# Storing the first chunk's scores by rows in an attention and expert kernel, and letting the first loads wait for their own rows

## The chip, the cores and the metric

The kernel runs on one core of one Trainium2 chip. The metric is the device time of one execution in microseconds (us). Times of the kernel before are the median of three runs.

## What is computed

Attention whose heads are mixed before and after the softmax, for 4 batches, 12 heads, 448 positions and 64 elements a head, and then a feed-forward product of two weight matrices with a gate between them:

```python
scores = scale * np.matmul(q, k.transpose(0, 1, 3, 2))
scores = np.einsum('bhij,hg->bgij', scores, w_pre)
scores = scores - np.max(scores, axis=-1, keepdims=True)
attn = np.exp(scores)
attn = attn / (np.sum(attn, axis=-1, keepdims=True) + 1e-09)
attn = np.einsum('bhij,hg->bgij', attn, w_post)
x = np.matmul(attn, v)              # then (b, i, h*d): 1792 x 768
h = x @ w_in                        # 768 x 2048
out = (h * np.clip(h + 3.0, 0.0, 6.0) / 6.0) @ w_out
```

## The kernel before

**Tiling.** Each batch's 448 rows of scores are cut into four chunks (120, 120, 120 and 90 rows, the last with two rows of padding). A chunk's scores are computed head pair by head pair with all rows on the partitions, but the mix of the heads wants the twelve heads of a few rows on the partitions. So the scores go through DRAM: a chunk is written there as `sd` (row, head, column), and read back as `T_all`, ten rows times twelve heads on the partitions. One load (line 491) brings twenty rows, two "steps" of ten; six loads make a chunk of 120 rows. A step is: first mix (PE, line 499), negated maximum (DVE, 506), exponent and sum (ACT, 507), scaling of the sum and of the exponents (POOL and DVE, 509 to 515), second mix (PE, 534), copy into the chunk's `A` (ACT and DVE, 543 and 545). When a chunk's `A` is full, it is multiplied with `v` (line 571), and two chunks together are the tokens of one pass of the experts' first product (line 769), which ends the start of the program.

**The first chunk.** `first_scores` (line 412) treats chunk 0 of batch 0 apart: each pair's two heads are copied out of PSUM by ACT (line 423) and DVE (line 424) into one buffer `S0` of all twelve heads, and each pair is stored by a transfer of its own, 120 rows of two heads (line 425). The load of step `s` lists the whole `sd` among what it reads, so every load of chunk 0 waits for all six stores.

**What runs beside it.** `w_in` comes in sixteen items of 768 KB (line 662), each decoded from 64-bit numbers by one pass on ACT (617) and DVE passes (620 to 632) before it is split into two halves of 16 bits. `v` comes in four loads. PE, when the planner sees it idle between 9 and 150 us of its own reckoning, is given filler matmuls on the identity (line 808).

**What sets the order.** All instructions are written down first as operations with an engine, a duration, what they read and write, and a priority; `Plan.schedule` (line 171) then places them one by one, each engine taking the operation of lowest priority value among those that are ready by its reckoning, and `Plan.run` (line 268) keeps the best of 128 such orders. An engine executes its list in order; so does SP, which issues every transfer here. An operation in another's `order` list may not start before that other one has started; one in its `succ` list, not before it has ended. Because the order is planned anew, a changed operation at the start can move rows anywhere in the program.

The store of a pair, and what a load of step `s` waits for:

```python
dma(CI * 3584, lambda: SP.dma_start(sd()[:, h:h + 2], S0()[:, h:h + 2]),
    [(S0, h), (S0, h + 1)], [(sd, pr)], at + 0.7)            # line 425
t_load[s] = dma(215040 * R, lambda: SP.dma_start(
    T_all()[4:4 + HR * R, slot], sd()[i0:i0 + 10 * R].rearrange("(u r) h j -> (r h) u j", u=2)),
    [sd, T_all], [T], s - 2.5)                               # line 491
```

Of the kernel before, what the change touches and what calls it, by code (L numbers as in the profile page):

```python
# [28 lines left out]
CI = 120  # L29
# [7 lines left out]
HR = G5 * H  # L37
# [10 lines left out]
LATE_W = 'P4', 'P5', 'P3'  # L48
HALF, W_AT, W_BY, EARLY, V_AT = 8, 20, 6, 1, 2
POST16 = 24  # L50
FILL_FROM, FILL_TO = 9, 150
WO_EARLY, WO_AT, WO_BY = 24, 72, 4
NH = S // 2
# [230 lines left out]
def body(ctx: ExitStack, tc: tile.TileContext, q4, kT, vj, wpre0, wpost0, ident0, w_in, w_out, outT):  # L284
    nc = tc.nc
    PE, ACT, DVE, POOL, SP = nc.tensor, nc.scalar, nc.vector, nc.gpsimd, nc.sync
# [19 lines left out]
    def buf(pool, shape, dt, tag, name, bufs=1, ring=True):  # L306

        g = rings.setdefault((id(pool), tag), Ring(bufs)) if ring else None
        return Buf(lambda: pool.tile(shape, dt, tag=tag, name=name, bufs=bufs), g)

    def const(shape, dt, name, pool=keep):
        return Buf(lambda: pool.tile(shape, dt, name=name))

    def act(dur, fn, r, w, prio):
        return plan.op("ACT", dur, fn, r, w, prio)

    def dve(dur, fn, r, w, prio, share=False):
        return plan.op("DVE", dur, fn, r, w, prio, share=share)

    def pool(dur, fn, r, w, prio):  # L320
        return plan.op("POOL", dur, fn, r, w, prio)

    def pe(dur, fn, r, w, prio, after=(), mode=0):
        return plan.op("PE", dur, fn, r, w, prio, after, 0, mode)

    def dma(nbytes, fn, r, w, prio, after=()):
        return plan.op("SP", 0.5, fn, r, w, prio, after, nbytes)
# [15 lines left out]
    def place(places):  # L343
        z = Buf(None)
        z.pool = places
        return z
# [53 lines left out]
    S0 = buf(apool, [CI, H, S], F32, "A", "s0", 2)  # L400

    def products(q, k, pr, at):

        def mm():
            for c, m in ((0, D), (D, CI - D)):
                for u in range(2):
                    r = slice(u * D, u * D + D)
                    PE.matmul(at[u]()[c:c + m], q()[r, pr, c:c + m], k()[r, pr % 3, :], start=True, stop=True)  # L408

        return mm  # L410

    def first_scores(pr, at):
        sd, q, k = s_dram[0, 0], qs[0, 0], ks[0, pr // 3]
        if pr % 3:
            ps = [place(singles) for u in range(2)]
            at2 = [lambda u=u: ps[u]()[:, :S] for u in range(2)]
        else:
            two = place(pairs)
            ps = [(two, 0), (two, 1)]
            at2 = [lambda u=u: two()[:, u, :S] for u in range(2)]  # L420
        pe(0.77, products(q, k, pr, at2), [(k, pr % 3), q], ps, at, mode=1)
        h = 2 * pr
        act(0.45, lambda: ACT.activation(S0()[:, h], at2[0]()[:CI], AF.Copy), [ps[0]], [(S0, h)], at + 0.5)
        dve(0.55, lambda: DVE.tensor_copy(S0()[:, h + 1], at2[1]()[:CI]), [ps[1]], [(S0, h + 1)], at + 0.5)
        dma(CI * 3584, lambda: SP.dma_start(sd()[:, h:h + 2], S0()[:, h:h + 2]), [(S0, h), (S0, h + 1)], [(sd, pr)], at + 0.7)


    s_dram, last_qk = {}, []
# [1 line left out]
    def scores(b, c, pr, at):  # L430
        n = CH[c]
        if pr == 0:
            s_dram[b, c] = Buf(lambda: dsc.tile([CI, H, S], F32, name=f"sd_{b}_{c}"))
        if (b, c) == (0, 0):
            return first_scores(pr, at)
        sd, q, k = s_dram[b, c], qs[b, c], ks[b, pr // 3]
        ps = place(pairs)
        last_qk[:] = [pe(0.77, products(q, k, pr, [lambda u=u: ps()[:, u, :S] for u in range(2)]), [(k, pr % 3), q], [ps], at, last_qk, mode=1)]
        st = buf(rot, [CI, 2, S], F32, "s", f"s_{b}_{c}_{pr}", 2)
        act(0.82, lambda: ACT.activation(st()[:n], ps()[:n, :, :S], AF.Copy), [ps], [st], at + 0.5)  # L440
        dma(n * 3584, lambda: SP.dma_start(sd()[:n, 2 * pr:2 * pr + 2], st()[:n]), [st], [(sd, pr)], at + 0.7)
# [33 lines left out]
    A, t_load = {}, {}  # L475

    def step(s):


        b, t = divmod(s, STEPS)  # L480
        c = min(t // 12, 3)
        t -= 12 * c
        if t % 2:
            t_load[s] = t_load[s - 1]
            return
        i0 = t * SI
        R = 2 if t < NST[c] - 1 else 1
        slot = s // 2 % NT_BUFS
        T = Buf(None, rings.setdefault(("T", slot), Ring(1)))
        sd = s_dram[b, c]  # L490
        t_load[s] = dma(215040 * R, lambda: SP.dma_start(
            T_all()[4:4 + HR * R, slot], sd()[i0:i0 + 10 * R].rearrange("(u r) h j -> (r h) u j", u=2)), [sd, T_all], [T], s - 2.5)
        ps = [place(mixed) for r in range(R)]

        def pre():
# [7 lines left out]
        pe(0.39 * R, pre, [T, wpre8], [*ps, (e, "pe")], s - 0.7, mode=1)  # L503
        eh, el = (buf(rot, [P, 2, S], F16, x, f"{x}_{s}", 2) if s >= POST16 else None for x in ("eh", "el"))
        for r in range(R):
# [8 lines left out]
        for r in range(R):  # L514
            pool(0.63, lambda r=r: POOL.tensor_scalar(e()[:, r], e()[:, r], rr()[:, r:r + 1], 1.0, op0=ALU.mult, op1=ALU.mult), [rr], [(e, r)], s + 0.6 + 0.3 * r)  # L515
            if s >= POST16:
                act(0.47, lambda r=r: ACT.activation(eh()[:, r], e()[:, r], AF.Copy), [(e, r)], [(eh, r)], s + 0.65 + 0.3 * r)  # L517
                pool(1.02, lambda r=r: POOL.tensor_tensor(el()[:, r], e()[:, r], eh()[:, r], op=ALU.subtract), [(e, r), (eh, r)], [(el, r)], s + 0.7 + 0.3 * r)  # L518
        if s < POST16:
            mix, dur = [(e, wpost_n)], 1.05  # L520
# [272 lines left out]
    T_all = const([P, NT_BUFS, 2, S], F32, "T_all", one)  # L793
# [28 lines left out]
    for C in range(1, 16):  # L822
        b, c = divmod(C, 4)
# [5 lines left out]
    for s in range(NS + 12):  # L829
# [3 lines left out]
        if s < NS:  # L833
            step(s)
        while todo and todo[0][0] - 2 <= s:
            at, _, b, c, pr = todo.pop(0)
# [17 lines left out]
        for C in range(16):  # L854
            b, c = divmod(C, 4)
# [282 lines left out]
```

## Time and profile before

| | |
|---|---|
| median of 3 runs | 815.24 us (813.91 to 818.32) |
| the profiled execution | 812.05 us |
| its span in the profile | 810.3 us |
| mean granted clock of TensorE | 0.994 |
| busy PE, DVE, ACT, POOL | 789.3, 599.0, 527.0, 370.3 us |
| bytes moved by DMA | 185.60 MB |

The span is the time between the first and the last instruction that the profile holds; what lies around it is part of the execution's time. Busy time of PE holds the 106 fillers, which compute nothing of the result. A row of the chain or of the timeline gives the start and the duration in us, the engine (SPq is SP's queue of DMA issues, where the duration is that of issuing), the line, the operation, and what it writes and reads.

### The profile page before, as it was taken

To read this page: it belongs to the slowest core of one execution; us is meant where nothing else is said; L and a number is where in the kernel's file an instruction comes from. 1 tells how busy PE (TensorE), PEld (TensorE's weight loads), DVE (VectorE), ACT (ScalarE), POOL (GpSimd) and SP (SyncE) were. 2 spreads that over 40 slices of the span, in tenths; PEclk is the share of its full clock that TensorE was granted. 3 is DMA by queue.
4 is the path that set the end of the run, shared out by engine and by line. 5 is a ranking of instruction groups with operands and counts; after the bars stand their busy time and mean duration, and the time that the engine had idled before them with its cause. 6 is when DMAs were issued, how large, how long until landed. Compare 5 with 4: busy or idle time off the path is not lost.

```text
span 810.3 us, 27770 instructions
## 1 busy us (share of the span) xinstructions
PE 789.3 (97%) x11642; PEld 635.8 (78%) x11642; DVE 599.0 (74%) x1185; ACT 527.0 (65%) x1043; POOL 370.3 (46%) x534
## 2 busy tenths in 40 slices
PE   8989999999999999999999999999999999999998
PEld 3554577667776777677777778798899999999998
DVE  5588898678759778896777976946676799888632
ACT  3467888897888878687877768747673783333200
POOL 2245697786787767576675647644300000000000
PEclk9999899999999999999999999999999999999999
DMA  7979996888688898999889878673497773654101
GB/s 258 282 247 314 304 279 193 256 281 242 213 263 251 255 304 267 298 294 279 271 247 313 287 253 255 220 208 96 135 362 245 245 249 106 184 158 144 35 20 51
DMA packets 111104, 185.60 MB, mean 229 GB/s; under 512 B 8692, under 2 KB 80468, under 8 KB 110980
## 3 DMA queue, kind: packets, MB, share of 16 engines
q1 hardware_dynamic: 110980, 183.84, 72.4%
q8 instruction: 91, 1.49, 0.8%
q14 instruction: 33, 0.27, 0.1%
HBM read 113.91 MB, written 69.90 MB: 227 GB/s over the span
## 4 chain that ended last, share of the span: by engine, by line
PE 67%; DMA 15%; DVE 8%; ACT 5%; issue 2%; POOL 2%; SPq 1%; ACTq 0%; DVEq 0%; POOLq 0%
PE single L1038 24%; PE single L769 19%; PE single L534 7%; PE single L571 6%; PE pair L408 5%; PE single L499 5%; DMA wo<-in_w_out 4%; DMA wi<-in_w_in 4%; DMA T_all<-sd 3%; DMA wsd_P<-WF 2%; DMA sd<-s 2%; DVE nb L506 2%; ACT e L507 2%; DVE A L543 1%; ACT s L440 1%
## 5 line engine op out<-in xcount | busy, mean ns | idle before, releaser
L769 PEld LDWEIGHTS <-wi 128*128 128x128 f16 x2304 | 213.3, 98 | 22.9 <-issue 16.9
L769 PE MATMUL single<-x,wi 128*128 128x208 f16 (+1 forms) x2304 | 227.1, 259 | 1.6 <-ACT e L507 1.5
L518 POOL TENSOR_TENSOR el<-e,eh 128x448 f16<-128x448 f32 x156 | 170.1, 1110 | 53.7 <-ACT eh L517 44.5
L515 POOL TENSOR_SCALAR e<-e,r 128x448 f32<-128x448 f32 x180 | 129.9, 731 | 30.6 <-DVE r L510 28.1
L1038 PEld LDWEIGHTS <-ws_P 128*128 128x128 f16 x1440 | 138.0, 98 | 0.0
L507 ACT ACTIVATE e<-single,nb 128x448 f32<-128x448 f32 x180 | 112.8, 635 | 22.9 <-DVE nb L506 22.5
L506 DVE TENSOR_REDUCE nb<-single 128x1 f32<-128x448 f32 x180 | 101.9, 613 | 15.4 <-PE single L499 15.2
L782 ACT ACTIVATE g<-single,three,uh 128x208 f32<-128x208 f32 (+1 forms) x128 | 68.7, 539 | 49.9 <-PE single L769 48.1
L517 ACT ACTIVATE eh<-e 128x448 f16<-128x448 f32 x156 | 87.5, 577 | 12.5 <-POOL e L515 11.8
L784 DVE SCALAR_TENSOR_TENSOR g<-g,six,single 128x208 f32<-128x208 f32 (+1 forms) x128 | 56.6, 443 | 51.3 <-ACT g L782 50.8
L408 PE MATMUL pair<-ks,qx 64*64 64x448 f32 x736 | 91.6, 566 | 2.1 <-ACT s L440 1.9
L440 ACT ACTIVATE s<-pair 120x896 f32<-120x896 f32 (+1 forms) x90 | 82.2, 913 | 14.5 <-PE pair L408 8.9
L499 PE MATMUL single<-T_all,wpre 64*64 64x448 f32 (+1 forms) x720 | 85.1, 551 | 4.0 <-DMA T_all<-sd 1.2
L571 PEld LDWEIGHTS single<-A,v 128*64 128x64 f32 x1536 | 74.0, 137 | 11.1 <-ACT e L507 3.4
L571 PE MATMUL single<-A,v 128*64 128x120 f32 (+1 forms) x1536 | 77.7, 261 | 1.4 <-ACT e L507 1.1
L534 PEld LDWEIGHTS <-eh 60*128 60x128 f16 x2496 | 66.3, 100 | 16.0 <-issue 13.8
L534 PE MATMUL single<-wpost_h,el 60*128 60x60 f16 x1248 | 71.4, 202 | 1.1 <-POOL el L518 1.1
L534 PE MATMUL single<-wpost_h,eh 60*128 60x60 f16 x1248 | 71.7, 202 | 0.8 <-DVE g L784 0.7
L534 PE MATMUL single<-wpost_l,eh 60*128 60x60 f16 x1248 | 71.3, 202 | 0.0
L509 POOL TENSOR_SCALAR sm<-sm 128x2 f32<-128x2 f32 (+1 forms) x92 | 24.7, 269 | 97.7 <-ACT e L507 93.3
L1038 PE MATMUL single<-gx_P,ws_P 128*128 128x224 f16 x720 | 69.3, 259 | 0.0
L1038 PE MATMUL single<-wg,ws_P 128*128 128x224 f16 x720 | 69.3, 259 | 0.0
(238 smaller groups left out, 1134.2 us busy)
## 6 DMA issues: line engine op xcount, KB each, us to landing
T_all<-sd SPq DMA_DIRECT2D x88, 420.0 KB, 6.3
sd<-s SPq DMA_DIRECT2D x72, 420.0 KB, 5.8
wi<-in_w_in SPq DMA_DIRECT2D x16, 768.0 KB, 7.7
wo<-in_w_out SPq DMA_DIRECT2D x24, 512.0 KB, 6.7
wsd_P<-WF SPq DMA_DIRECT2D x42, 256.0 KB, 5.0
wP<-wsd_P SPq DMA_DIRECT2D x36, 256.0 KB, 4.3
gd<-g SPq DMA_DIRECT2D x32, 240.0 KB, 4.0
sd<-s SPq DMA_DIRECT2D x24, 315.0 KB, 4.9
```

Of the source, the lines that this page charges most:

```text
L408: PE.matmul(at[u]()[c:c + m], q()[r, pr, c:c + m], k()[r, pr % 3, :], start=True, stop=True)
L440: act(0.82, lambda: ACT.activation(st()[:n], ps()[:n, :, :S], AF.Copy), [ps], [st], at + 0.5)
L499: PE.matmul(ps[r]()[64 * u:64 * u + 64, :S], wpre8()[rows], T_all()[rows, slot, u], start=True, stop=True)
L506: dve(0.53, lambda r=r: DVE.tensor_reduce(nb()[:, r:r + 1], ps[r]()[:, :S], axis=AX.X, op=ALU.max, negate=True), [ps[r]], [(nb, r)], s + 0 ...
L507: act(0.62, lambda r=r: ACT.activation(e()[:, r], ps[r]()[:, :S], AF.Exp, bias=nb()[:, r:r + 1], accum_out=sm()[:, r:r + 1]), [ps[r], (nb, ...
L515: pool(0.63, lambda r=r: POOL.tensor_scalar(e()[:, r], e()[:, r], rr()[:, r:r + 1], 1.0, op0=ALU.mult, op1=ALU.mult), [rr], [(e, r)], s + ...
L517: act(0.47, lambda r=r: ACT.activation(eh()[:, r], e()[:, r], AF.Copy), [(e, r)], [(eh, r)], s + 0.65 + 0.3 * r)
L518: pool(1.02, lambda r=r: POOL.tensor_tensor(el()[:, r], e()[:, r], eh()[:, r], op=ALU.subtract), [(e, r), (eh, r)], [(el, r)], s + 0.7 + 0 ...
L534: PE.matmul(out, x()[rows, r, js], z()[rows], start=(i == 0), stop=(i == len(mix) - 1))
L571: PE.matmul(ps()[u * D:(u + 1) * D, k:k + n], v()[:, jc, g * D:(g + 1) * D], a()[:, jc * H + g, :n], start=(jc == 0), stop=(jc == NJ - 1))
L769: PE.matmul(pv(), wi_g[g]()[:, w, f0, cc, :], x()[:, z, cc, :n], start=(cc == 0 and i == 0), stop=(cc == 5 and i == 2))
L1038: PE.matmul(ps()[:, :NH], w_view(w, y, 2 * m + i)[:, f], g(x)[:, f, :], start=(i == 0 and f == 0 and (y, x) == (0, 0)), stop=(i == 1 and f ...
```

## The change

The scores of chunk 0 are stored when half of the heads are there (`PG = 3` pairs, six heads), in three transfers by rows: 0 to 20, 20 to 60 and 60 to 120. There are still six stores, of 20, 40 and 60 rows twice. The load of each step reads only those pieces of `sd` whose rows it needs: load 0 the two 20-row stores, loads 2 and 4 the two of 40 rows, the rest those of 60. The stores of 40 and 60 rows are held behind the start of load 0 (`ROWS_S = 0`), and `ROWS_AT` gives the three kinds of store their priorities.

```diff
+ROWS_S, PG, ROWS, ROWS_AT = 0, 3, ((0, 20), (20, 60), (60, CI)), (-9, -2.4, -1.4)
...
+    row_ops = []
+
     def first_scores(pr, at):
...
-        dma(CI * 3584, lambda: SP.dma_start(sd()[:, h:h + 2], S0()[:, h:h + 2]), [(S0, h), (S0, h + 1)], [(sd, pr)], at + 0.7)
+        if (pr + 1) % PG:
+            return
+        z = slice(2 * (pr + 1 - PG), 2 * pr + 2)
+        for i, (x, y) in enumerate(ROWS):
+            o = dma((y - x) * 1792 * 2 * PG, lambda x=x, y=y: SP.dma_start(sd()[x:y, z], S0()[x:y, z]), [(S0, k) for k in range(z.start, z.stop)], [(sd, (i, pr // PG))], ROWS_AT[i] + 0.1 * pr)
+            row_ops.append((i, o))
...
         t_load[s] = dma(215040 * R, lambda: SP.dma_start(
-            T_all()[4:4 + HR * R, slot], sd()[i0:i0 + 10 * R].rearrange("(u r) h j -> (r h) u j", u=2)), [sd, T_all], [T], s - 2.5)
+            T_all()[4:4 + HR * R, slot], sd()[i0:i0 + 10 * R].rearrange("(u r) h j -> (r h) u j", u=2)),
+            [sd if (b, c) != (0, 0) else (sd, (i, pr)) for i, (x, y) in enumerate(ROWS) for pr in range(6 // PG) if (b, c) != (0, 0) or x < i0 + 10 * R and y > i0] + [T_all], [T], s - 2.5)
+        for i, o in row_ops if s == ROWS_S else ():
+            if i:
+                t_load[s].order.append(o)
+                o.n += 1
```

What this does to the order, at two places. First SP's list from the first `w_in` item on, before (`sd` is the scores in DRAM, `qx` the queries of a chunk, `wi` an item of `w_in`):

```order
L662 DMA wi_123<-in_w_in 128x768
L425 DMA sd_0_141<-s_130 120x896 x6
L491 DMA T_all<-sd_0_141 120x2x448 x3
L398 DMA qx_1_239<-in_q 128x720
L398 DMA qx_2_284<-in_q 128x720
L662 DMA wi_286<-in_w_in 128x768
L457 DMA v_296<-in_vj 128x768
L491 DMA T_all<-sd_0_141 120x2x448
```

and now, over the same work:

```order
L675 DMA wi_123<-in_w_in 128x768
L432 DMA sd_0_155<-s_130 20x2688 x2
L499 DMA T_all<-sd_0_155 120x2x448
L432 DMA sd_0_155<-s_130 40x2688 x2
L432 DMA sd_0_155<-s_130 60x2688 x2
L399 DMA qx_1_236<-in_q 128x720
L399 DMA qx_2_265<-in_q 128x720
L675 DMA wi_267<-in_w_in 128x768
L499 DMA T_all<-sd_0_155 120x2x448 x3
L449 DMA sd_1_329<-s_1_0_327 120x896
L449 DMA sd_1_329<-s_1_1_341 120x896
L465 DMA v_355<-in_vj 128x768
```

The first load stands alone after two stores, and four stores, two loads of queries and an item of `w_in` stand between it and the next three loads, of which the first two went out with it before; the first stores of chunk 1's scores now come ahead of `v`.

Second, DVE's list after the first `w_in` item, before (`nb` is the maximum of a step, `r` its reciprocal sum, `A_0` chunk 0's result, `wist` the maximum of a `w_in` item):

```order
L681 SCALAR_TENSOR_TENSOR wi_233<-WF,wir_223,wi_233 128x768
L506 TENSOR_REDUCE nb_288<-single_154 128x1
L506 TENSOR_REDUCE nb_288<-single_156 128x1
L506 TENSOR_REDUCE nb_304<-single_87 128x1
L506 TENSOR_REDUCE nb_304<-single_126 128x1
L506 TENSOR_REDUCE nb_318<-single_135 128x1
L510 RECIPROCAL r_324<-sm_301 128x2
L506 TENSOR_REDUCE nb_318<-single_137 128x1
```

and now:

```order
L694 SCALAR_TENSOR_TENSOR wi_233<-WF,wir_219,wi_233 128x768
L519 TENSOR_REDUCE nb_269<-single_157 128x1
L519 TENSOR_REDUCE nb_269<-single_87 128x1
L523 RECIPROCAL r_279<-sm_273 128x2
L556 TENSOR_SCALAR A_0_324<-single_135 128x48x10
L633 TENSOR_SCALAR WF,wist_362<-WF 128x768
L519 TENSOR_REDUCE nb_367<-single_145 128x1
L519 TENSOR_REDUCE nb_367<-single_137 128x1
```

The six maxima of three loads stood in one run before the second item of `w_in`; now the first load's two maxima and its copy into `A` come before that item, and the other loads' maxima after its first pass. In PE's list 23 fillers stand between the broadcast of the first item's maximum and the first load's matmuls, where there were 39; then come 20 fillers, the second mix of the first load, and three groups of chunk 1's scores with six fillers after each of the first two, before the second load's matmuls. The fillers are 109 in all, for 106.

## Rows read from the trace of the kernel before

**Rows 1.** Busy time by stretch: engines' us (instructions), TensorE clock, DMA share, GB/s.

```profile
40.00:60.00 20.00, 17.91 (x198) 10.18 (x192) 17.16 (x45) 13.00 (x22) 9.87 (x20) 0.91 0.72 244
60.00:100.00 40.00, 39.12 (x403) 20.98 (x403) 33.10 (x80) 31.35 (x56) 23.44 (x46) 0.91 0.98 310
100.00:120.00 20.00, 19.52 (x315) 13.82 (x308) 19.58 (x35) 16.70 (x38) 18.43 (x26) 1.00 0.92 282
120.00:810.00 690.00, 675.69 (x10456) 574.24 (x10454) 508.44 (x981) 450.55 (x900) 309.67 (x426) 1.00 0.71 220
```

**Rows 2.** Timeline of PE, 15 to 45 us: start, duration, work.

```profile
15.98 8.59 PE L808 MATMUL single<-ident 128*128 128x512 bf16 x39
24.51 0.98 PE L499 MATMUL single<-T_all,wpre 64*64 64x448 f32 x8
...
25.96 0.98 PE L499 MATMUL single<-T_all,wpre 64*64 64x448 f32 x8
...
29.67 0.98 PE L408 MATMUL pair<-ks,qx 64*64 64x448 f32 x8
...
35.26 0.98 PE L408 MATMUL pair<-ks,qx 64*64 64x448 f32 x8
...
36.92 2.00 PE L534 MATMUL single<-wpost_n,e 60*128 60x60 f32 x32
```

**Rows 3.** The chain of waits, 0 to 130 us: start, duration, what.

```profile
5.64 7.21 DMA wi<-in_w_in
12.86 6.70 DMA sd<-s
...
20.45 7.09 DMA T_all<-sd
...
116.66 7.54 PE single L769 x72
```

**Rows 4.** Timeline of SP's queue, 0 to 60 us: start, duration of issuing.

```profile
7.68 6.32 SPq L425 DMA_DIRECT2D sd<-s  x6
19.57 1.31 SPq L491 DMA_DIRECT2D T_all<-sd  x3
```

**Rows 5.** Busy time by stretch, columns as in rows 1, around the stores.

```profile
14.00:15.00 1.00, 0.02 (x1) 0.02 (x1) 0.97 (x3) 0.00 (x0) 0.00 (x0) 1.00 0.93 369
...
18.00:19.00 1.00, 1.00 (x6) 0.43 (x5) 0.28 (x1) 0.69 (x1) 0.96 (x2) 1.00 0.06 25
...
20.00:21.00 1.00, 1.00 (x7) 0.43 (x5) 0.30 (x1) 0.00 (x0) 0.00 (x0) 1.00 0.38 45
...
22.00:23.00 1.00, 1.00 (x6) 0.49 (x5) 0.00 (x0) 0.00 (x0) 0.00 (x0) 1.00 0.98 224
...
16.40:20.40 4.00, 4.00 (x20) 1.85 (x19) 2.76 (x8) 0.94 (x1) 1.91 (x4) 1.00 0.15 60
```

**Rows 6.** Landing times: the loads of T issued by 22 us; a small load.

```profile
DMA to landing us min/median/max: 4.1/5.6/7.1
...
ident<-in_ident SPq DMA_DIRECT2D x1, 32.0 KB, 3.6
```

**Rows 7.** Timeline of DVE, 8 to 36 us: the last copies; the second `w_in` item.

```profile
8.32 0.62 DVE L424 COPY s<-single 120x448 f32<-120x448 f32 x1
...
9.53 1.38 DVE L424 COPY s<-single 120x448 f32<-120x448 f32 x2
...
34.20 0.94 DVE L620 TENSOR_SCALAR_CACHE_REDUCE WF<-WF 128x768 f32<-128x768 f32 x1
```

**Rows 8.** DVE's groups by line, 20 to 41.2 us: busy us, mean ns; idle before.

```profile
L506 DVE TENSOR_REDUCE nb<-single 128x1 f32<-128x448 f32 x8 | 4.7, 617 | 6.0 <-PE single L499 6.0
L543 DVE TENSOR_SCALAR A<-single 128x480 f32<-128x480 f32 x3 | 2.0, 651 | 2.2 <-PE single L534 2.2
```

**Rows 9.** Timeline of ACT, 30 to 40 us: a score copy, a `w_in` pass.

```profile
30.72 0.92 ACT L440 ACTIVATE s<-pair 120x896 f32<-120x896 f32 x1
31.54 0.91 ACT L617 ACTIVATE WF<-wi 128x768 f32<-128x768 f32 x1
```

## The prediction

> **What bounds the kernel now.** I first read the busy time in stretches. After 120 us PE is busy 675.69 of 690 us [rows 1], so what is late there is late at the end. Before 120 us no engine is full throughout: from 40 to 120 DVE is busy 69.84 of 80 us, the DMA engines 0.72 to 0.98 [rows 1], and PE's high shares hold filler matmuls. So the time that the first 120 us take is passed on almost whole, and inside it DVE and the DMA engines are the nearest things to a limit. PE's first 20 us here are no work of the result: 39 fillers take 8.59 us up to 24.57 [rows 2].
>
> The chain of waits gives the order of the start: the load of the first w_in item, then the last store of chunk 0's scores, then the loads of T [rows 3]. SP's own rows show why: six stores are issued over 6.32 us from 7.68, and SP then stands until 19.57, when all six have landed; three loads of T go out in one run [rows 4]. The slices show what that wait is. Alone in the queue the stores hold 0.93 of the 16 engines at 369 GB/s; from 16.4 to 20.4 the share is 0.15, and in 18 to 19 it is 0.06, one engine of sixteen finishing alone [rows 5]. The three loads land 4.1, 5.6 and 7.1 us after their issues [rows 6], and the first two loads' matmuls run from 24.51 and 25.96 [rows 2]. The first product of the experts, which ends this phase, starts at 116.66 [rows 3].
>
> **The change, part by part.** My sum is made against the profiled execution: span 810.3, its time 812.05, which is 3.19 us under the median of 815.24; I add the difference in the span to the median.
>
> *The first store and load.* A half (six heads) is ready when its DVE copies are. Those of pairs 0 to 2 end at 8.32 + 0.62 = 8.94, all at 9.53 + 1.38 = 10.91 [rows 7]. The change issues the scale's constants ahead of the second keys and puts their small reductions between the copies; as an estimate I add one copy with its gap (half of the row of two, 0.69): second half out at 11.6. A 20-row transfer (215 KB) is no row of this trace. It lies between a 32 KB load (3.6 us to landing) and a 420 KB load into an empty queue (4.1) [rows 6]; nothing excludes a slower one, and a 420 KB store behind a full queue took 6.70 [rows 3]. I take 4.1, since the queue has run empty by then. So load 0 goes out at 15.7 (15.2 to 18.3) in place of 19.57 and lands at 19.8. But PE cannot start it before its 23 fillers are through: 8.59/39 = 0.22 us each from 15.98, that is 21.0. Step 0's matmuls come at 21.0, **3.5 us earlier**.
>
> *What SP holds back.* While SP waits for load 0, the 40- and 60-row stores, both query loads and w_in item 1 stand behind it. From 15.7 the DMA engines have: 1.0 us until data flow (issue at 19.57, share 0.38 in the slice 20 to 21 [rows 4, 5]), load 0 of 430 KB at 224 GB/s 1.9 [rows 5], the four stores left, 2.15 MB at 369 GB/s, 5.8, two queries and w_in (1.52 MB, at the same rate) 4.1, load 2 1.9, and the 1.2 us that load 0's 4.1 leave after its 1.0 + 1.9. So load 2 lands at 31.6; before, second of the three that SP issued in 1.31 us, it went out near 20.0 and landed 5.6 us later, at 25.6. That is **6.0 us later**, where all three loads came together before.
>
> *PE behind it.* After step 0 come 20 fillers (4.4 us), its sixteen second-mix matmuls (2.0 for a load's worth, the row at 36.92 [rows 2]), and three groups of chunk 1's scores of 0.98 us with six fillers after each of the first two. That is 21.0 + 1.0 + 4.4 + 2.0 + 2.9 + 2.6 = 33.9 for step 2 in place of 25.96, **7.9 us later**. The first score groups move the other way: 28.4 for 29.67 and 30.7 for 35.26 [rows 2], 4.5 us earlier for the second.
>
> *DVE.* When it starts on w_in item 1 (34.20 before [rows 7]) it had done six maxima at 617 ns. Now it has done two, and one copy of A at 651 ns [rows 8]: 3.7 against 1.9, **1.8 us behind**. That decode starts at about the same time: ACT's first pass over item 1 now stands behind the copies of two score groups, 31.7 + 0.92, and takes 0.91 [rows 9], so 33.5. The hiding work is the 10.2 us in which DVE does nothing between 40 and 120, and 5.6 us of free DMA between 40 and 60 [rows 1]. If that cover were gone, the 1.8 would be the price, and two loads of T that are still owed (3.8 us) would come on top.
>
> *Changes I cost at nothing.* The twelve copies into SBUF stay, and so do six transfers; the bytes are the same; the waits of the first loads on fewer stores cost no instruction on PE or DVE. The fillers are 109 in place of 106 (0.7 us of PE in which it has nothing else). From about step 24 on, the planner's new order does the same work in another sequence on all engines; the 14.3 us in which PE is idle after 120 [rows 1] are what it can win or lose there, and I take nothing for it and 3 us either way for the range.
>
> *Sum.* Step 0 is 3.5 early, but neither PE nor DVE has work that follows from it until step 2, which is 7.9 late; score groups of chunk 1 are early by up to 4.5; DVE's 1.8 are mostly made good in its 10.2 of idle time. I put the rest at +1: **816 us**, own range 811 to 820.
>
> **The rivals.**
> *The lead carries through (faster).* Chunk 1's scores come up to 4.5 us earlier, and its first loads now stand behind five w_in items instead of six in SP's order. If chunk 1's loads set the pace to 120 us, the 4.5 reach the end: 810.7. For it: the T loads and score stores are on the chain. Against it: so is w_in, whose decode on DVE is not earlier.
> *The held-back stores decide (slower).* The wait of load 0 on SP, with 2.15 MB of stores behind it, makes steps 2 and 4 late, and DVE has no room to catch up: 1.8 + 3.8 = 5.6, 821. It decides from the point where DVE's idle time between 40 and 120 falls by less than the 1.8 it owes. For it: DVE at 19.58 of 20 us from 100 on and DMA at 0.98 from 60 to 100 [rows 1]. Against it: the idle time before.
> *Few rows, few engines.* A transfer ends with its slowest engine (the 0.06 slice), and 0.93 is about 15/16: 120 rows already leave an engine out. If 20 and 40 rows ran on ten engines, the busiest would carry (0.43 + 0.86)/10 + 1.29/15 MB = 215 KB in place of 2.58/15 = 172 KB; at 369/15 = 24.6 GB/s that is 1.8 us more before load 2, on top of my +1: 818. The Trainium skill, DMA: Bandwidth & Descriptors, in its section on why a DMA increments its semaphore by 16, says that a transfer takes the largest number of engines up to 16 that divides its slowest dimension, which would be 15 for 120 and 60 rows and 10 for 20 and 40. By that rule the trace agrees for 120 rows (0.93); no run so far shows 20 or 40.
> *The change does not do what it says.* If load 0 still waited for other stores, it would go out near 19.6 and only the reordering would be left: 815. SP's order speaks against it, with the load between the 20- and the 40-row stores.
>
> **How the numbers follow.** Forecast 0.50, lead carries 0.18, held-back stores 0.18, few engines 0.09, no effect 0.05. A measurement of this kernel tells about 0.5% (4.1 us) from no change. Faster: 0.18, and 0.04 of the forecast's own spread: 0.22. Slower: 0.18, 0.05 of the forecast's spread and 0.02 of few engines: 0.25. Same: the rest, 0.53. The range 809 to 822 takes in the faster and the slower case with 1 to 2 us of spread, and leaves out about a fifth.
>
> **What would show it.** Right: load 0 issued near 15.7, step 0's matmuls near 21, load 2 landing after 30, step 2 near 34, the experts' first product within 2 us of 116.66. A 20-row store that lands 6 us after issue, or load 2 before 28, would break the middle steps. Wrong as a whole: that first product comes more than 4 us earlier or later, or PE's idle time after 120 us changes by more than 4 us, so that the later order decides and not the start.

## The result and the profile after

The changed kernel is slower: median 824.85 us (821.61 to 826.76, 4 runs) beside 815.17 (813.91 to 818.32, 4 runs), a ratio of 1.0105 with the interval 1.0068 to 1.0141. The forecast was 816.0 with a range of 809 to 822. Each ratio here sets fast runs against fast runs of the kernel before taken beside them; a few runs of e7, e10, e13 and e15, e7's profiled one among them, were slow ones (over 1.5% above the fastest of their kernel) and count only in the medians of the table below. The profiled execution took 826.76 us, span 825.0, mean clock 0.983.

The change does what it says. SP's timeline after (start, duration of issuing; [rows 4] before):

```profile
8.74 3.42 SPq L432 DMA_DIRECT2D sd<-s  x2
14.78 0.33 SPq L499 DMA_DIRECT2D T_all<-sd  x1
15.16 4.17 SPq L432 DMA_DIRECT2D sd<-s  x4
19.38 4.23 SPq L399 DMA_DIRECT2D qx<-in_q  x2
25.68 4.10 SPq L499 DMA_DIRECT2D T_all<-sd  x3
```

Load 0 goes out 4.8 us earlier. PE's timeline after shows what follows (start, duration, work, in brackets the wait ahead of it; [rows 2] before):

```profile
20.27 0.98 PE L512 MATMUL single<-T_all,wpre 64*64 64x448 f32 x8
...
25.60 2.00 PE L547 MATMUL single<-wpost_n,e 60*128 60x60 f32 x32
32.20 1.76 PE L409 MATMUL pair<-ks,qx 64*64 64x448 f32 x8 [4.60 <-DMA qx<-in_q]
...
35.99 0.98 PE L409 MATMUL pair<-ks,qx 64*64 64x448 f32 x8
...
39.10 0.93 PE L512 MATMUL single<-T_all,wpre 64*64 64x448 f32 x8
```

Step 0 is 4.2 us earlier, and then PE stands for 4.60 us until the queries of chunk 1 have landed. Step 2 runs at 39.10, 13.1 us later than before. The chain of waits now passes through these queries, and the experts' first product, at 116.66 before [rows 3], comes at 127.75 (first row: the chain; second: PE's timeline):

```profile
19.38 12.79 DMA qx<-in_q
```

```profile
127.75 3.45 PE L782 MATMUL single<-x,wi 128*128 128x240 f16 x32
```

So 11.1 us of the 14.7 between the two profiled spans lie ahead of the first product. The two executions lie 5.0 us further apart than the medians, so the 3.6 behind it can't be told from the spread of executions: that stretch is 693.6 us before and 697.3 after, and from 690.2 to 698.5 in the seven runs below that play back the changed kernel's order with an edit (e1, e3, e4, e5, e9, e10, e11). PE's idle time from 120 us on is 9.57 us in the row that answers to the last of [rows 1], less than the 14.3 before:

```profile
120.00:810.00 690.00, 680.43 (x10507) 570.74 (x10504) 515.29 (x995) 459.86 (x918) 319.54 (x440) 1.00 0.72 222
```

**PE's account of the start.** PE executes its list in order, so its first product comes when idle time, fillers and real work ahead of it are through. Busy time by stretch (columns as in [rows 1]), all of PE's work and then the fillers' line alone, first of before:

```profile
7.00:40.00 33.00, 31.27 (x264) 14.62 (x260) 20.43 (x47) 13.61 (x29) 6.22 (x13) 1.00 0.89 280
40.00:116.70 76.70, 73.25 (x874) 41.83 (x867) 66.72 (x153) 57.76 (x107) 48.60 (x85) 0.93 0.91 291
...
7.00:40.00 33.00, 15.89 (x68) 6.09 (x68) 1.00 0.89 280
40.00:116.70 76.70, 10.44 (x38) 3.18 (x38) 0.93 0.91 291
```

and of after:

```profile
7.00:40.00 33.00, 27.90 (x181) 10.92 (x174) 12.82 (x33) 8.90 (x15) 3.29 (x7) 0.90 0.81 230
40.00:127.70 87.70, 81.28 (x964) 48.83 (x960) 68.91 (x164) 63.82 (x122) 50.06 (x92) 0.92 0.88 272
...
7.00:40.00 33.00, 17.32 (x73) 6.77 (x74) 0.90 0.81 230
40.00:127.70 87.70, 9.50 (x37) 2.87 (x37) 0.92 0.88 272
```

The first row of each gives idle time as the stretch less PE's busy time, and real work as busy time less the fillers'. By 40 us PE had done 31.27 - 15.89 = 15.4 us of real work before, and 10.6 after. From 40 to the first product it was idle 3.5 of 76.7 us before, 6.4 of 87.7 after. With the first 7 us, which are the same, the 11.0 us are 6.3 of idle time, 0.5 of fillers, and 4.2 because the same work (1032 matmuls and 1035) ran longer: the granted clock is 0.90 in place of 1.00 up to 40 us, and 0.92 in place of 0.93 after it. After 40 us PE was idle for only 3.5 us in the kernel before, and the fillers stand in its list whatever is late. So what it has not done by 40 us is late at the first product, as long as the fillers and the clock behind it stay as they are.

### The profile page after: what moved, and what is told of

Its sections match the earlier page's. It is cut to its first block, busy times and chain, and to the rows that moved or that the text cites. A ratio compares the mean times of both kernels' runs of the same rounds, so it can differ in the third digit from the quotient of the medians.

```text
span 825.0 us, 27771 instructions
## 1 busy us (share of the span) xinstructions
PE 799.4 (97%) x11645; PEld 640.5 (78%) x11645; DVE 595.6 (72%) x1185; ACT 527.4 (64%) x1043; POOL 370.7 (45%) x534
## 4 chain that ended last, share of the span: by engine, by line
PE 73%; DMA 14%; DVE 7%; ACT 3%; issue 2%; SPq 1%; POOL 0%; ACTq 0%; DVEq 0%; POOLq 0%
PE single L1051 23%; PE single L782 19%; PE single L584 8%; PE single L547 7%; PE pair L409 7%; PE single L512 6%; DMA sd<-s 4%; DMA v<-in_vj 3%; DMA wo<-in_w_out 2%; DMA qx<-in_q 2%; DMA T_all<-sd 1%; DVE nb L519 1%; DMA wi<-in_w_in 1%; DVE WF L641 1%; DVE A L556 1%
## 5 line engine op out<-in xcount | busy, mean ns | idle before, releaser
L782 PEld LDWEIGHTS <-wi 128*128 128x128 f16 x2304 | 213.2, 98 | 19.6 <-issue 13.2
L512 PE MATMUL single<-T_all,wpre 64*64 64x448 f32 (+1 forms) x720 | 89.1, 554 | 5.4 <-DMA T_all<-sd 4.1
L584 PEld LDWEIGHTS single<-A,v 128*64 128x64 f32 x1536 | 76.7, 140 | 12.1 <-ACT eh L530 4.2
L584 PE MATMUL single<-A,v 128*64 128x120 f32 (+1 forms) x1536 | 80.8, 266 | 0.8 <-DVE g L797 0.5
L522 POOL TENSOR_SCALAR sm<-sm 128x2 f32<-128x2 f32 (+1 forms) x92 | 22.4, 244 | 117.2 <-ACT e L520 110.9
```

Source lines behind the costliest of these rows:

```text
L512: PE.matmul(ps[r]()[64 * u:64 * u + 64, :S], wpre8()[rows], T_all()[rows, slot, u], start=True, stop=True)
L584: PE.matmul(ps()[u * D:(u + 1) * D, k:k + n], v()[:, jc, g * D:(g + 1) * D], a()[:, jc * H + g, :n], start=(jc == 0), stop=(jc == NJ - 1))
L782: PE.matmul(pv(), wi_g[g]()[:, w, f0, cc, :], x()[:, z, cc, :n], start=(cc == 0 and i == 0), stop=(cc == 5 and i == 2))
```

## The experiments

Except where a kernel is said to be planned, the planner is left out and every engine plays back the recorded order of one of the two kernels, edited at the place shown. "First product" and "profiled" are those of the profiled execution. The kernel before was run again beside each group of runs: its median was 814.28 beside e1 to e4, 815.27 beside e5 to e8, 815.22 beside e9 to e12 and 816.09 beside e13 to e16, so kernels of different groups are compared by their ratios.

| run | median us (range; runs) | ratio to before [95%] | profiled | first product |
|---|---|---|---|---|
| before | 815.17 (813.91 to 818.32; 4) | 1 | 812.05 | 116.7 |
| changed | 824.85 (821.61 to 826.76; 4) | 1.0105 [1.0068, 1.0141] | 826.76 | 127.7 |
| e1 new order, pair stores | 822.20 (819.93 to 829.42; 6) | 1.0115 [1.0068, 1.0161] | 825.03 | 127.2 |
| e2 old order, row stores | 819.64 (817.17 to 826.62; 12) | 1.0081 [1.0053, 1.0110] | 818.39 | 124.3 |
| e3 queries first | 818.31 (812.90 to 822.89; 12) | 1.0046 [1.0011, 1.0080] | 817.69 | 120.8 |
| e4 no hold | 829.70 (825.34 to 832.95; 6) | 1.0187 [1.0142, 1.0231] | 830.71 | 134.9 |
| e5 even rows | 821.27 (813.48 to 824.08; 12) | 1.0065 [1.0036, 1.0095] | 821.39 | 126.5 |
| e6 before, queries first | 812.58 (806.79 to 817.73; 12) | 0.9960 [0.9929, 0.9990] | 817.63 | 118.7 |
| e7 before, other draws | 821.07 (811.88 to 834.06; 12) | 1.0064 [1.0031, 1.0097] | | |
| e8 changed, other draws | 822.76 (818.39 to 828.48; 6) | 1.0103 [1.0064, 1.0141] | 818.39 | 119.2 |
| e9 late gap filled | 827.59 (819.79 to 830.88; 6) | 1.0140 [1.0089, 1.0191] | 829.74 | 129.5 |
| e10 both gaps filled | 824.13 (817.96 to 831.07; 7) | 1.0109 [1.0069, 1.0148] | 817.96 | 125.9 |
| e11 even rows, queries first | 817.43 (813.76 to 825.45; 12) | 1.0051 [1.0021, 1.0081] | 816.78 | 121.5 |
| e12 before, queries and w_in first | 818.07 (811.91 to 823.50; 12) | 1.0023 [0.9990, 1.0056] | 814.49 | 117.9 |
| e13 changed, half of w_in | 817.80 (812.05 to 825.20; 12) | 1.0010 [0.9982, 1.0038] | 818.60 | 122.9 |
| e14 before, half of w_in | 810.52 (808.25 to 814.97; 12) | 0.9941 [0.9916, 0.9966] | 810.40 | 113.1 |
| e15 before, third draws | 823.19 (815.08 to 829.34; 12) | 1.0078 [1.0043, 1.0113] | 818.24 | 114.9 |
| e16 changed, third draws | 826.45 (824.92 to 833.90; 6) | 1.0160 [1.0115, 1.0206] | 833.02 | 128.9 |

### Stores or order: e1 and e2

e1 gives the changed kernel's order the six pair stores back; e2 puts the row stores into the order of before.

```diff
e1  on SP, after's order
- sd 20x2688 x2 | T load 0 | sd 40x2688 x2 | sd 60x2688 x2
+ sd 120x896 x6 | T load 0
e2  on SP, before's order
- sd 120x896 x6 | T loads 0, 2, 4 | qx x2
+ sd 20x2688 x2 | T load 0 | sd 40x2688 x2 | sd 60x2688 x2 | T loads 2, 4 | qx x2
```

> Every engine keeps the order of the changed kernel; only the six row stores are put back to one store of 120 rows for each head pair. Theory S (the held-back stores: 2.15 MB of stores go out behind the first load, so the queries of chunk 1 land at 32.2 in place of about 29 and PE stands still from 27.6 to 32.2): the queries land by 25, the first product of the experts comes back from 127.8 to 120 or less, time 815 to 818. Theory O (the planner's new order after 60 us, above all the stores of chunk 3's scores around 97 to 106, costs the time): the first product stays at 126 to 130 and the time at 823 to 826.

> Every engine keeps the order of the kernel before; only the six stores become the row stores, two of 20 rows, the first load, then two of 40 and two of 60 rows. Theory S: the second load and the queries behind it are late by 5 us or more, the first product moves from 116.7 to 122 or later, time 821 or more. Theory O: what is late at 30 us is made good by 70 us, as the loads of chunk 1 at 62.2 in both kernels suggest, and the time is 815 within 3.

Both are slower than before, by about as much as the change itself (1.0115 and 1.0081 beside 1.0105): each half costs by itself, in its own way, and neither theory met all its numbers. In e1 theory S failed: the queries landed by 25 as it said, but the first product stayed at 127.2, in theory O's range. There load 0 went out at 19.00, step 0 waited and ran at 23.09, and step 2 stood behind the fillers, the second mix and three score groups at 37.41: the new list of PE is made for an early load 0. So the wait for the queries is not the only way to lose these microseconds. In e2 the first product, 124.3, is theory S's; the median lies a little under its 821. Loads 2 and 4 stood behind the held-back stores. PE's timeline of e2:

```profile
23.47 0.98 PE L512 MATMUL single<-T_all,wpre 64*64 64x448 f32 x8
24.39 0.60 PE L815 MATMUL single<-ident 128*128 128x512 bf16 x2
31.08 3.68 PE L512 MATMUL single<-T_all,wpre 64*64 64x448 f32 x16 [6.09 <-DMA T_all<-sd]
```

The load that went out at 14.00 brought nothing, because that list keeps its 39 fillers ahead of step 0, and PE then waited 6.09 us for the next two.

### The queries' place: e3

```diff
on SP, after's order
  sd 20x2688 x2
+ qx x2
  T load 0 | sd 40x2688 x2 | sd 60x2688 x2
- qx x2
```

> The changed kernel's order with one move: the two loads of queries (720 KB) go out ahead of the first load of T, while the DMA engines are idle, in place of behind the four stores. Theory S: the queries land by 20, PE's wait of 4.6 us at 27.6 goes, the first product comes 4 to 8 us earlier than 127.8, time 817 to 821. Theory O: PE's wait goes as well but is made good later anyway; the first product stays within 2 of 127.8 and the time at 823 to 826.

Theory S met its numbers. The ratio fell from 1.0105 to 1.0046, which is 0.59 of the 1.05 per cent or some 4.8 us, and the first product came 6.9 us earlier. PE's timeline of e3 has no wait at the first score group, and step 2 waits for its load instead:

```profile
27.64 0.98 PE L409 MATMUL pair<-ks,qx 64*64 64x448 f32 x8
...
35.14 0.98 PE L512 MATMUL single<-T_all,wpre 64*64 64x448 f32 x8 [1.91 <-DMA T_all<-sd]
```

PE's account of e3, as above:

```profile
7.00:40.00 33.00, 30.88 (x207) 11.53 (x199) 16.01 (x39) 11.77 (x23) 3.49 (x8) 0.95 0.89 275
40.00:120.80 80.80, 73.29 (x945) 44.05 (x941) 66.70 (x158) 61.37 (x116) 49.39 (x90) 1.00 0.90 276
...
7.00:40.00 33.00, 17.17 (x74) 6.75 (x74) 0.95 0.89 275
40.00:120.80 80.80, 8.93 (x35) 2.82 (x35) 1.00 0.90 276
```

Of the 6.9 us only 1.9 are idle time and 0.7 fillers; 4.3 are real work that ran at a higher clock, 78.1 us in place of 82.4. So the greater part of what the queries' place gave back is the clock, which stayed at 1.00 from 40 us on in this execution.

### The hold and the rows: e4 and e5

```diff
e4  on SP, after's order
- sd 20x2688 x2 | T load 0 | sd 40x2688 x2 | sd 60x2688 x2
+ sd 20x2688 x2 | sd 40x2688 x2 | sd 60x2688 x2 | T load 0
e5  after's order
- ROWS = ((0, 20), (20, 60), (60, CI))
+ ROWS = ((0, 30), (30, 75), (75, CI))
```

> The changed kernel's order with one move: the stores of 40 and 60 rows are no longer held behind the first load but issued right after those of 20 rows, so the first load is issued only after them but still waits for its own rows alone. Theory S: DMA does not stand idle from 12 to 16, queries land by 28, PE's wait shrinks to under 1 us, time 817 to 821 although the first load lands later (22 to 24). Theory O: 823 to 826.

> The changed kernel's order, with the rows cut at 30 and 75 in place of 20 and 60: stores of 30, 45 and 45 rows. Theory K (a store runs on as many engines as the number of its rows allows, 10 for 20 and 40 rows, 15 for 30, 45 and 60): the DMA share while the first stores are alone rises from 0.51 to 0.9 or more, the first load is issued no later than 14.78 plus 0.5 although its stores carry half as much again, and the queries land 1 to 3 us before 32.2; time 821 to 824. Rival (the share is low because a transfer of few long rows has little in flight, whatever the number of engines): share stays under 0.65, the first load is issued 1 us or more later, the queries land at 32 or later; time 824 to 827.

e4 is the slowest of all, slower than both theories had it: load 0 waits for the two small stores alone, but was issued at 17.21 behind the others and landed 11.7 us later. PE's timeline of e4:

```profile
28.95 1.77 PE L512 MATMUL single<-T_all,wpre 64*64 64x448 f32 x8 [8.39 <-DMA T_all<-sd]
```

The hold is needed: here a load that waited for little was still served behind the data that was issued ahead of it. In e5 the first stores carry half as much again, and load 0 still went out at 14.85 (14.78 after). Slices while the second of the two first stores is alone in the queue (columns as in [rows 1]), first after with 20 rows, whose 215 KB are all that moves:

```profile
12.00:13.00 1.00, 1.00 (x6) 0.43 (x5) 0.86 (x6) 0.81 (x1) 0.00 (x0) 1.00 0.51 108
13.00:14.00 1.00, 1.00 (x6) 0.39 (x4) 0.97 (x4) 0.00 (x0) 0.00 (x0) 1.00 0.51 108
```

then e5 with 30, 322 KB and the last of the store before:

```profile
12.00:13.00 1.00, 1.00 (x6) 0.41 (x5) 0.86 (x5) 0.74 (x1) 0.00 (x0) 1.00 0.63 161
13.00:14.00 1.00, 1.00 (x6) 0.48 (x5) 0.84 (x2) 0.17 (x1) 0.00 (x0) 1.00 0.77 183
```

The count of packets shows how a store is divided. A row of a store, six heads, is one packet of 10.75 KB; in the trace after ten of them start at 12.6 to 13.2 us and the other ten at 13.3 to 13.9, and then 10 packets under 512 B close the transfer. In e5 15 such packets do. The views of 13.6 to 15 us, after and then e5:

```profile
DMA packets 10, 0.00 MB, mean 0 GB/s; under 512 B 10, under 2 KB 10, under 8 KB 10
...
DMA packets 21, 0.06 MB, mean 46 GB/s; under 512 B 15, under 2 KB 15, under 8 KB 15
```

So the store of 20 rows went out ten rows at a time, in two rounds, and that of 30 rows fifteen at a time, in as many rounds. Of theory K's numbers the share of 0.9 was missed (0.63 and 0.77, since a slice holds the gaps between the rounds); the issue of load 0 and the time came as it said, and the queries landed even earlier. The rival missed all of its numbers but the share in the first slice.

PE's timeline of e5:

```profile
28.25 0.98 PE L409 MATMUL pair<-ks,qx 64*64 64x448 f32 x8 [0.45 <-DMA qx<-in_q]
```

The queries landed 4 us earlier, behind the same transfers in the same order. The held-back stores are 90 rows twice in place of 100, 0.22 MB less; at the 258 GB/s that the engines moved from 15 to 28 us after, that is an estimated 0.8 of the 4 us. The total moved does not account for the rest: from 15 to 22 us it is 1.83 MB after and 1.89 MB in e5. It goes with the division by rows; how the bytes of the later stores lay on the single engines no view here shows. Yet the wait of 4.60 us being gone but for 0.45, the first product came only 1.2 us earlier: from 40 us on the real work took 70.2 us in e5 and 64.4 in e3, at a granted clock of 0.90 and 1.00. That put the next question: what happens after 98 us.

### The late gap and the clock: e9 and e10

Between 98 and 122 us the changed kernel loses time again. PE's timeline after shows a wait for a score copy and then long matmuls, and two slices show the clock (last columns: granted clock, DMA share, GB/s):

```profile
106.54 1.34 PE L409 MATMUL pair<-ks,qx 64*64 64x448 f32 x8 [2.01 <-ACT s L448]
107.80 3.67 PE L547 MATMUL single<-wpost_n,e 60*128 60x60 f32 x32
...
113.10 7.15 PE L584 MATMUL single<-A,v 128*64 128x120 f32 x96
```

```profile
105.00:106.00 1.00, 0.00 (x0) 0.00 (x0) 1.00 (x2) 0.43 (x1) 1.00 (x1) 1.00 0.93 377
...
116.00:117.00 1.00, 1.00 (x14) 1.00 (x12) 0.96 (x2) 0.54 (x2) 0.85 (x1) 0.50 0.85 265
```

ACT's copy in turn had waited 2.31 us for a store of scores that took 8.44 us to land in the chain.

```diff
e9   on PE, after's order
- fillers x8  | scores at 106.54
+ fillers x16 | scores
e10  as e9, and
  second mix of step 0 at 25.60
+ fillers x19
  scores at 32.20
```

> Every engine plays back the changed kernel's order; the filler of TensorE that stands ahead of the score group at 106.54 has 16 matmuls in place of 8, some 1.9 us more, which fills the wait of 2.01 us there. Theory C (clock): what the changed kernel loses a second time between 98 and 122 us is the granted clock of 0.50 from 107 to 117 us after that wait, not the wait: with the gap filled the clock stays at 1.00, the 96 attention matmuls take 5.1 and not 7.2 us, the first expert product stands 4 to 5 us earlier, near 123, and the median is 820 (818 to 822). Theory W (waits): the score copies wait for the landing of stores, whatever the clock: first product within 1.5 us of 127.7, median 825 (823 to 827).

> As the one before, and 19 more filler matmuls, some 4.5 us, stand ahead of the first score group of chunk 1, where TensorE waited from 27.6 to 32.2 us for the queries. Theory C: the clock stays at 1.00 from 29 to 35 us too, the score groups at 32.2 take 0.98 and not 1.76 us, but the queries still land at 32.2: first product a further 0 to 3 us earlier than with the late gap alone, near 121.5, median 818.5 (816 to 821). Theory W: within 1.5 us of 127.7, median 825 (823 to 827).

The ratios, 1.0140 and 1.0109, stand beside 1.0105: theory C's numbers failed, though the clock did what it said. In e9 it stayed at 1.00 from 98 to 129 us, and the first product still came at 129.5 (e9's second score group, unlike the changed kernel's, ran at half clock). In the profile of e10 it is 1.00 throughout from 20 to 40 and from 100 to 130 us, and the real work ahead of the first product, with the first 7 us, took 82.9 us in place of 88.2. But that product came only 1.8 us earlier. Fillers took 32.1 us in place of 26.8, most of it where PE had stood idle up to 40 us; and from 40 us on PE was idle for 8.3 us in place of 6.4.

### Bytes in the queue: e13 and e14

Both are planned; the plans' costs are left as they were, so the orders are those of the two kernels.

```diff
- dma(786432, lambda: SP.dma_start(raw(), w_in[fc]), ...)
+ part = slice(0, NCC * P // 2 if 2 <= fc <= 10 else NCC * P)
+ dma(786432, lambda: SP.dma_start(raw()[:, part], w_in[fc][:, part]), ...)
...  the decode of these items reads the loaded half twice
```

> The changed kernel in its own order, with half the bytes of nine w_in loads (items 2 to 10, 393 KB less each, 3.5 MB in all); the decode reads the half that was loaded twice, so the second half of the columns of these weights is left out. The count of every engine's instructions stays. Theory W (waits for transfers): TensorE has the same work to do before its first expert product in every kernel; what the changed kernel lost after 40 us is its 6.4 us of waits there and the clock that fell with them, because loads and stores queue behind each other. With fewer bytes these waits shrink to about the 3.5 us that the kernel before has: first product 120 to 123, median 818 (815 to 821). Theory B (bytes set the pace of the whole start): 32.9 MB have moved by the first product in both kernels, so 3.5 MB less bring it 11 to 13 us forward, to 115, and the median to 812. Theory O (only the order counts): within 2 us of 127.7, 825 (822 to 827).

> The same in the kernel before: half the bytes of the w_in items 2 to 10, the second half of the columns of these weights left out. Theory W: TensorE there waits only 3.5 us between 40 and 116.7 and its filler stands in its order whatever the loads do, so the first product comes 1 to 4 us earlier at most, 113 to 116, and the median is 813 (810 to 815). Theory B: 3.5 MB of 33.1 MB less, first product near 104, median 803 (800 to 806).

Theory W met its numbers for the first product and the time in both. In e13 the early wait for the queries stayed (4.80 us), while PE's idle time from 40 us to the first product fell from 6.4 to 4.4 us and the clock there rose to 0.96; the first product came 4.9 us earlier. In e14, with nine items halved as well, it came 3.6 earlier. So theory B falls: the start of neither kernel goes by the total of bytes. But the late waits are only a small part of what the change costs. With the bytes halved in both, the first products still lie 9.8 us apart (11.1 with all of them), and the ratios 1.0010 and 0.9941 lie 0.7% apart (1.05% before).

### A plan drawn anew: e7, e8, e15 and e16

All four are planned; only the random draws of the planner's trials differ.

```diff
- rnd = random.Random(k)
+ rnd = random.Random(k + 1000)     # e7, e8; k + 2000 in e15, e16
- (rnd.uniform(-JITTER, JITTER) if k else 0.0)
+ rnd.uniform(-JITTER, JITTER)
```

> The kernel before, planned anew with 32 other random draws of the priorities: same operations, another order. If any new plan costs some microseconds in the start, since the order before is a lucky one, the first product comes at 120 to 128 and the time is 818 to 825. If the loss belongs to the row stores, it stays within 3 of 116.7, time 813 to 818.

> The changed kernel planned with the same 32 other draws. If the loss belongs to the row stores and the loads held behind them, the queries again land after 30, the first product comes at 124 to 130, time 821 to 828. If the changed kernel's order was an unlucky one, the first product comes at 115 to 121 and the time is 813 to 819.

> The kernel before, planned with a third series of random draws. If the plan on record was a lucky one among equals, this is slower than it too, by 2 to 8 us: 820 (817 to 823). If the second series was an unlucky one, 815 (812 to 817).

> The changed kernel, planned with the same third series. If the change itself costs its place of the queries whatever the plan, it is 2 to 7 us above the kernel before with the same draws: 825 (821 to 829), with TensorE waiting 4 to 5 us for the queries of chunk 1 near 32 us. If the plans alone differ, both come out within 2 us of each other.

The times of e7 and e8, of e15 (its median lies just over its range) and of e16 are what was expected if the plan on record is a lucky one and the change costs in any plan. The plan on record of the kernel before is the best of three: the others are 0.64% and 0.78% slower. The changed kernel's three are 1.0105, 1.0103 and 1.0160. Pair by pair with the same draws the change costs 0.4% and 0.8%; of these the first is no more than the intervals of the two ratios, the second is clear of them. PE's wait for the queries is in every plan of the change, here e8 and then e16, and the profile of e15, the kernel before, has none:

```profile
32.25 1.76 PE L409 MATMUL pair<-ks,qx 64*64 64x448 f32 x8 [4.82 <-DMA qx<-in_q]
```

```profile
32.05 1.76 PE L409 MATMUL pair<-ks,qx 64*64 64x448 f32 x8 [5.07 <-DMA qx<-in_q]
```

But the wait does not fix the first product. In e8's profile that came at 119.2, not at the 124 to 130 that was expected of a loss by the row stores. PE's account of e8:

```profile
7.00:40.00 33.00, 28.18 (x184) 11.08 (x180) 12.51 (x32) 9.37 (x16) 3.30 (x7) 0.90 0.78 227
40.00:119.20 79.20, 69.22 (x892) 41.52 (x885) 69.00 (x158) 60.91 (x116) 45.97 (x86) 1.00 0.96 303
...
7.00:40.00 33.00, 17.84 (x72) 6.76 (x72) 0.90 0.78 227
40.00:119.20 79.20, 4.37 (x17) 1.33 (x17) 1.00 0.96 303
```

By 40 us PE had done 10.3 us of real work, no more than in the changed kernel (10.6). From there on it was idle for 10.0 us, but its list holds 4.4 us of fillers in place of 9.5, and the clock was 1.00 in place of 0.92. This was the fastest of e8's six executions, 818.39 for a median of 822.76. A plan's loss need not sit in the start either: e15's first product came at 114.9, earlier than before.

Among the executions of each kernel a longer time tends to go with a lower granted clock, and so it does between kernels: the mean is 0.989 in the four executions of the changed kernel, 0.995 in the twelve of e3, 0.981 in the six of e16, and 0.993 in those of the kernel before beside e3. So a part of the change's cost lies with the clock; how large a part of the medians no run here separates.

### Looking for a better kernel: e6, e11, e12

```diff
e6   on SP, before's order
  sd 120x896 x6
+ qx x2
  T loads 0, 2, 4
- qx x2
e12  as e6, and w_in item 1 behind the queries
e11  after's order, the edits of e3 and e5 together
```

> The kernel before with one move: the two loads of queries (720 KB) go out ahead of the first loads of T, while SP waits for the six stores and the DMA engines run empty from 17 to 20.5. If the start is bound by what the DMA engines bring in from 20 to 40 us, the fourth to sixth loads of T and the third w_in item land 1.5 to 2.5 us earlier and the first product moves from 116.7 to 114 to 116: 812 to 814. If DVE and PE set the pace there, the first product stays within 1 of 116.7 and the time within 1.5 of the kernel before.

> The kernel before, every engine in its own order, but SP issues both query loads and the w_in load that followed ahead of the first three T loads, in the stretch in which its queue moved little (about 15 to 19.5 us). If the idle stretch of the queue is free to take, the T loads land no later and the 3 us of SP behind them are gained: 812 (809 to 815). If the 393 KB of the w_in load stands in the way of the T loads, step 0 is 1 us or more later and it is 815 (813 to 818).

> The changed kernel's order with both query loads ahead of T0's load, and rows 30, 45 and 45 in place of 20, 40 and 60. Theory C: both early delays are gone or smaller, and if the clock stays at 1.00 after 100 us it gives what the run with the queries first gave or a little less: 817 (814 to 820); if the clock falls there, 820 and a first product 4 to 5 us later than 120.8. Theory Q (the place of the queries is all there is): 818 (816 to 820) whatever the clock does.

e6 is 0.4% faster than the kernel before, with an interval that only just leaves out no change: it uses the stretch in which the queue stood nearly empty (0.15 in [rows 5]). Its profile does not show where the gain lies: the first product came at 118.7, not at 114 to 116, in the second slowest of its twelve executions. e12 takes one load too many into that stretch: the first loads went out 0.3 us later, step 0 waited 1.60 us, at 26.45, and its time can't be told from the kernel before. e11 adds nothing that can be measured to e3. Its clock fell to 0.50 at 105 to 107 us, and the first product is still within 0.7 us of e3's, so theory Q met its numbers and theory C did not.

## Why the prediction was wrong

- **Load 0 and step 0: right.** Issued at 14.78 (forecast 15.7), landed 4.4 us later (4.1), matmuls at 20.27 (21.0).
- **What SP holds back: a term that was too small.** I let the four held-back stores, 2.15 MB, drain at the 369 GB/s of the six pair stores, 5.8 us, and counted the queries only as bytes ahead of load 2. By that sum the queries' 0.74 MB would have landed near 27.6, ahead of the score groups. Measured were 258 GB/s from 15 to 28 us, 3.35 MB, about what load 0, the stores and the queries hold together (3.32); with the forecast's 1.2 us to landing that makes 29. They landed at 32.2, 12.79 us after their issue, and at 28.2 with 45 and 45 rows (e5). So as an estimate the rate took some 1.5 us and the division by rows some 3.
- **The rival "few rows, few engines"** had the mechanism, with too small a price (1.8 us forecast; of the 4 us that e5 gave back to the queries some 3 are the division by rows) and a chance of 0.09. Thirty rows took no longer than twenty, 161 to 183 GB/s against 108. By the rule cited there (the Trainium skill, DMA: Bandwidth & Descriptors, on why a DMA increments its semaphore by 16), which makes it fifteen engines for 30 rows and ten for 20, two rows each, the trace agrees: 15 closing packets and 10.
- **PE behind it.** The score groups were to be earlier, at 28.4 and 30.7; they came at 32.20 and 35.99, later than before. Step 2 was forecast at 33.9 and came at 39.10: 4.6 us of wait, and matmuls at half clock.
- **DVE: not the limit.** Its first pass over `w_in` item 1 came at 38.78 (34.20 before), after a wait of 10.45 us for ACT's pass (DVE's timeline after, below). That it had 10 us of room was true and did not help.
- **What bounds the kernel, and the cover in the sum: the step that failed.** The sum let a step 2 that is 7.9 us late cost +1, since "neither PE nor DVE has work that follows from it until step 2" and "PE's high shares hold filler matmuls". That was right up to 40 us only, where fillers are 15.89 of PE's 31.27 us. After it they are 10.4 of 76.7 us, at fixed places in the list, and idle time is 3.5, so the 4.8 us of real work that PE had not done by 40 were not made good: the first product came 11.1 us later. The granted clock, which fell to half after PE's waits, stands nowhere in the sum; longer work is 4.2 of the 11.0 us.
- **The order after step 24: taken at nothing.** The profiles can't tell 3.6 us behind the first product from spread. But a plan drawn anew costs 5 to 6 us in the kernel before, so nothing was too little.
- **The held-back stores rival** forecast 821 for its mechanism and missed who waits: the queries and not DVE.

```profile
38.78 0.95 DVE L633 TENSOR_SCALAR_CACHE_REDUCE WF<-WF 128x768 f32<-128x768 f32 x1 [10.45 <-ACT WF L630]
```

The first mark that the forecast set for being wrong as a whole, a first product more than 4 us later, is what came. By the numbers the second came too, PE's idle time after 120 us changed by 4.7 us; but it fell, so it is not where the time went.

Shown is that 11.1 of the 14.7 us of the profiled loss lie ahead of the first product, with the rest inside the spread; that the queries' place is worth 0.59% in the changed kernel (e3; in its profile the greater part is clock); that their wait comes in each of its plans; and that with other rows nearly all of that wait goes (e5). That this wait alone makes the loss is not shown, and e1, e5 and e8 speak against it: the first product was late without it and nearly on time with it. The rest, 0.46% in e3, is no more than what new draws cost the kernel before (0.64% and 0.78%); that it has that cause is argued, not shown. Which plan's feature makes the one on record better stays open, and so does why the store of scores at 97 us took 8.44 us to land.

## What to carry to other kernels

When a transfer is held back, list everything that the same queue issues behind it, compute when each of those lands at the rate of this transfer's own shape, and look for the engine that meets each of them next; here the first store was early and the queries paid. Before a delay is called covered, subtract fillers from the busy time of the engine that works through a fixed list, see how much idle time is left later, and ask what a wait will do to the granted clock. Where a planner redraws the whole order, plan the kernel before with other draws too, so that the change is told from the plan.

## What was not expected of the hardware

- Transfers of few long rows were slow: a 20-row store of 215 KB, alone in the queue, went out in two rounds of ten packets and held 0.51 of the engines at 108 GB/s; one of 30 rows moved at 161 to 183 GB/s and let the next load go out at the same time.
- A load that waits for two small stores alone, issued behind four larger ones, landed 11.7 us later (e4).
- After PE had stood still from 27.6 us the granted clock was 0.50, 1.2 GHz, from 29 to 35 us, though PE worked again from 32.2 (two slices after, below). After the 2.01 us wait at 104.5 it was 0.50 from 107 to 117 us of unbroken work; after a wait of 1.91 us at the same place in e3 it stayed at 1.00.

```profile
29.00:30.00 1.00, 0.00 (x0) 0.00 (x0) 0.00 (x0) 0.00 (x0) 0.00 (x0) 0.50 0.81 251
...
34.00:35.00 1.00, 1.00 (x3) 0.33 (x3) 0.00 (x0) 0.92 (x1) 0.00 (x0) 0.50 0.98 217
```
